# Attention results kept with 128 following positions in the partitions: fewer stores, longer loads, shorter shifted copies

## The chip, the cores and the metric

The kernel runs on one core of one Trainium2 chip. The metric is device time in microseconds (us) of one launch; the core's engines are TensorE (PE, its weight loads PEld), VectorE (DVE), ScalarE (ACT), GpSimd (POOL) and SyncE (SP), which here only issues DMAs.

## What is computed

Eight batches of eight heads, 576 positions, head dimension 64. Heads 0 to 3 attend to the last 32 positions, heads 4 to 7 to every fourth of the last 128. The results, 4608 tokens of 512 numbers, go through a mixture of eight experts in which each expert takes at most 576 tokens, assigned in the order of the sorted logits.

```python
scores = scale * np.matmul(q, k.transpose(0, 1, 3, 2))
rel = pos[:, None] - pos[None, :]
mask_plain = (rel >= 0) & (rel < 32)
mask_dil = (rel >= 0) & (rel < 128) & (rel % 4 == 0)
attn = softmax(np.where(mask, scores, -1e9))          # plain for h < 4, dilated for h >= 4
x = np.matmul(attn, v).transpose(0, 2, 1, 3).reshape(4608, 512)
logits = x @ w_gate                                    # greedy assignment, 576 tokens an expert
out[mask] = np.maximum(x[mask] @ w1[e], 0.0) @ w2[e]
```

## The kernel before

The launch has two parts. `attention` works through 32 units (class `Unit`): a batch has two kinds (0 plain, 1 dilated, whose sequence is stored as four runs of 144 positions, so that its window is also 32 following places), a kind two units of two heads. The sequence is cut into NB = 9 chunks of 64 positions. Per unit, `scan` (L447, L451) finds maxima on TensorE, VectorE reduces them (L398), `scores` (L458, L463) forms the scores, ScalarE takes the exponent (L417) into E, `values` (L470) multiplies by v, and `weigh` (L476 to L478) divides on VectorE into the tile xs. Head a of the unit lies in partitions 64a to 64a+63 of xs, with the nine chunks side by side. `banks` then transposes xs on TensorE (L519), copies the transposed results into xt (L264 on ScalarE, L524 for the very last) and feeds the gate's logits (L544; L608 and L610 in `tokens` for the last batch) and the first counts of the routing (`R.choose`: L840 to L850; coarse counts L726, L731).

`load` and `load_values` bring q, k and v in on SP's queue, with two sets of tiles taken in turn by the batches. v goes into partitions 64 to 127; `shift_v` (L274, L276) copies it to partitions 0 to 63 as two shifted copies, on GpSimd after the first batch, so that one matmul sees a chunk and the 32 places ahead of it.

`stores` (L491) writes xs to the scratch tensor xd in device memory: 2 DMAs a batch for kind 0, 20 for kind 1, since the dilated runs end inside chunks and each head half needs its own DMA. All of these are issued by SP, in program order, among the loads. SP's DMAs use eight landing semaphores in turn, and a DMA that reuses one waits until the eighth DMA before it has landed (`DMAHW0` to `DMAHW7` among the program's waits).

The order of the instructions on each engine is made at build time: `Schedule.run` simulates the engines with the costs that stand in the code (in ns) and due times (`P_U` a unit, and constants such as `B_V`, `B_K`), and writes each engine's program in the order that comes out. The three PSUM accumulators px are a `Pool` of three, shared by `values`, the transposes and the logits.

`moe` follows. It begins with `search_alone` (L804 and on), a chain between VectorE and TensorE that needs all counts; its tiles take memory of the attention's, so its first instruction also waits for all stores. The experts' matmuls (L1266, L1308) fill the rest.

Of the kernel before, what the change touches and what calls it, by code (L numbers as in the profile page):

```python
# [8 lines left out]
F32 = mybir.dt.float32  # L9
# [32 lines left out]
NS, B_E, DIRECT = (2, 2), 3000, 7  # L42
# [195 lines left out]
def attention(tc, ctx, C, load_const, T, xd, Lt, R):  # L238
# [11 lines left out]
    KT = [[pk.tile([128, 2, 32 + S], F32, name=f"k{x}{s}") for s in range(2)] for x in range(2)]  # L250
# [6 lines left out]
    XS = [ring(pk, [128, NB, 2, D], F32, f"xs{x}", NS[x]) for x in range(2)]  # L257
# [53 lines left out]
    def borders(kind, s, eng):  # L311
# [3 lines left out]
        def fn():  # L315
            e.memset(KT[kind][s][:, :, :32], 0.0)
            e.memset(VT[kind][s][:32, 0].rearrange("p h d -> p (h d)"), 0.0)
# [7 lines left out]
    def load(b, kind, part=None):  # L325
# [10 lines left out]
        lk = sp(1, lambda: nc.sync.dma_start(KT[kind][s][:, ix, 32:], k[b][:, ix]), load.old, nb, b)  # L336
# [15 lines left out]
    def load_values(b, kind):  # L352
# [3 lines left out]
        for part in range(2):  # L356
            eng = "POOL" if b else ("DVE", "ACT")[part]
            f = {"ACT": act, "DVE": nc.vector.tensor_copy, "POOL": nc.gpsimd.tensor_copy}[eng]
            ready["V", kind, b].append(op(eng, {"ACT": 2300, "DVE": 1700, "POOL": 2450}[eng],
                                          lambda part=part, f=f: shift_v(b, kind, part, f), [ld, ready["b", kind, s]],  # L360
                                          -4 * b * P_U))
# [3 lines left out]
    class Unit:  # L365


        def __init__(self, u):
# [10 lines left out]
            self.K = KT[kind][s][:, ui]  # L379
# [7 lines left out]
        def build(self):  # L387
# [39 lines left out]
            for g in range(2):  # L427
                c0, c1 = self.gr[g]
                px = Buf(PV)
                d = self.op("PE", 135 * (c1 - c0), lambda c0=c0, c1=c1, px=px: self.values(c0, c1, px.tile),  # L430
# [3 lines left out]
                x = self.op("DVE", 780, lambda c0=c0, c1=c1, px=px: self.weigh(c0, c1, px.tile, rec, xs),  # L434
# [31 lines left out]
        def values(self, c0, c1, px):  # L466
            px = px[:, :5 * (D + 1)].rearrange("p (c x) -> p c x", c=5)
            for c in range(c0, c1):
                for a in range(2):
                    nc.tensor.matmul(px[64 * a:64 * a + 64, c - c0], self.E[:, c, 64 * a:64 * a + 64],  # L470
                                     self.V[:, c, self.ui + 2 * a], start=True, stop=True)

        def weigh(self, c0, c1, px, rec, xs):
            m = c1 - c0
            px = px[:, :5 * (D + 1)].rearrange("p (c x) -> p c x", c=5)
            nc.vector.tensor_scalar(rec[:, c0:c1], px[:, :m, D], 1e-9, None, op0=OP.add)  # L476
            nc.vector.reciprocal(rec[:, c0:c1], rec[:, c0:c1])
            nc.vector.tensor_tensor(xs[:, c0:c1, self.ui], px[:, :m, :D], rec[:, c0:c1, None].to_broadcast([128, m, D]),  # L478
                                    op=OP.mult)
# [960 lines left out]
```

## Time and profile before

| | us |
|---|---|
| median of 3 runs (lowest, highest) | 720.73 (717.96, 721.19) |
| the profiled execution, its time | 728.06 |
| its span in the trace | 726.3 |
| attention until the last result is weighed | 0 to 217.3 |
| from there to the search's first instruction | 217.3 to 231.1 |
| search, first lists and gathers | 231.1 to 257.2 |
| experts | 257.2 to 726.3 |

Over the span TensorE is busy 90%, VectorE 66%, ScalarE 40%, GpSimd 27%. The granted clock of TensorE is given as a share of full speed; in the trace it is either full (2.4 GHz) or half (1.2 GHz), so a mean between says how long it was half. Idle time of an engine stands in brackets with what ended it.

### The profile page before, as it was taken

To read this page: it belongs to the slowest core of one execution; us is meant where nothing else is said; L and a number is where in the kernel's file an instruction comes from. 1 tells how busy PE (TensorE), PEld (TensorE's weight loads), DVE (VectorE), ACT (ScalarE), POOL (GpSimd) and SP (SyncE) were. 2 spreads that over 40 slices of the span, in tenths; PEclk is the share of its full clock that TensorE was granted. 3 is DMA by queue.
4 is the path that set the end of the run, shared out by engine and by line. 5 is a ranking of instruction groups with operands and counts; after the bars stand their busy time and mean duration, and the time that the engine had idled before them with its cause. 6 is when DMAs were issued, how large, how long until landed. Compare 5 with 4: busy or idle time off the path is not lost.

```text
span 726.3 us, 18691 instructions
## 1 busy us (share of the span) xinstructions
PE 651.2 (90%) x7447; PEld 558.5 (77%) x7449; DVE 477.3 (66%) x1551; ACT 288.9 (40%) x610; POOL 193.9 (27%) x231
## 2 busy tenths in 40 slices
PE   6879888787893389999999999999999999999995
PEld 4767776666772359879979988988988988988984
DVE  5566566657743878978959978978977973833300
ACT  4545443342340147457523524523533534434210
POOL 5362533432400033364320311221121041121011
PEclk7899999998796599999999999999999999999998
DMA  9995585784532168489712711622441374123001
GB/s 236 272 232 163 156 220 159 179 197 111 131 80 54 45 196 174 111 260 225 232 54 68 246 51 52 197 102 66 151 147 52 131 254 152 60 75 100 1 23 43
DMA packets 67095, 99.07 MB, mean 136 GB/s; under 512 B 8000, under 2 KB 36416, under 8 KB 67008
## 3 DMA queue, kind: packets, MB, share of 16 engines
q1 hardware_dynamic: 57664, 72.71, 35.7%
q0 software_dynamic: 9344, 25.17, 13.0%
q8 instruction: 58, 0.95, 0.6%
q14 instruction: 29, 0.24, 0.1%
HBM read 72.69 MB, written 18.87 MB: 126 GB/s over the span
## 4 chain that ended last, share of the span: by engine, by line
PE 62%; DVE 15%; issue 14%; DMA 4%; SPq 2%; POOL 2%; ACT 1%; POOLq 0%; DVEq 0%
PE ph L1266 18%; PE py L1308 17%; PE pS L463 5%; PE px L470 4%; DMA k<-in_kp 4%; PE px L519 2%; PE px L544 2%; PE ptx L1229 2%; PE pz L739 2%; PE pS L458 2%; PE pm L451 1%; SPq L491 1%; PE py L1311 1%; PE py L1313 1%; DVE hb L1286 1%
## 5 line engine op out<-in xcount | busy, mean ns | idle before, releaser
L1308 PE MATMUL py<-w2h,hb 128*128 128x512 f32 x512 | 171.1, 399 | 0.0
L1266 PE MATMUL ph<-xh,w1h 128*128 128x256 f32 (+1 forms) x512 | 138.0, 300 | 0.0
L1266 PE MATMUL ph<-xl,w1h 128*128 128x256 f32 (+1 forms) x512 | 136.7, 298 | 0.0
L1266 PE MATMUL ph<-xh,w1l 128*128 128x256 f32 (+1 forms) x512 | 135.9, 296 | 0.0
L1308 PEld LDWEIGHTS py<-w2h,hb 128*128 128x128 f32 x512 | 96.1, 188 | 19.2
L1308 PE MATMUL py<-w2l,hb 128*128 128x512 f32 x256 | 99.9, 390 | 0.0
L1098 ACT ACTIVATE hb<-ph 128x256 fp32r<-128x256 f32 (+2 forms) x192 | 59.6, 345 | 89.3 <-PE ph L1266 87.0
L1334 POOL DMA_INDIRECT out<-y,idx x40 | 39.9, 997 | 197.1 <-ACT y L1098 138.3
L1266 PEld LDWEIGHTS ph<-xh,w1h 128*128 128x128 f32 x512 | 91.8, 190 | 0.5
L1266 PEld LDWEIGHTS ph<-xh,w1l 128*128 128x128 f32 x512 | 91.7, 190 | 0.1
L1266 PEld LDWEIGHTS ph<-xl,w1h 128*128 128x128 f32 x512 | 91.4, 190 | 0.1
L417 ACT ACTIVATE E<-pS 128x384 f32<-128x384 f32 x96 | 46.5, 490 | 89.4 <-PE pS L463 79.3
L1286 DVE SCALAR_TENSOR_TENSOR hb<-ph,hb 128x320 fp32r<-128x320 f32 (+1 forms) x128 | 57.1, 453 | 28.1 <-ACT hb L1098 25.0
L1098 ACT ACTIVATE y<-py 128x512 f32<-128x512 f32 (+1 forms) x40 | 23.8, 596 | 102.1 <-PE py L1308 90.3
L463 PE MATMUL pS<-q,k 128*64 128x64 f32 x1152 | 58.6, 244 | 3.1 <-issue 3.1
L1215 POOL DMA_INDIRECT xg<-xd,idx x40 | 41.6, 1040 | 51.9 <-PE ph L1266 31.4
L1308 PEld LDWEIGHTS py<-w2l,hb 128*128 128x128 f32 x256 | 48.2, 188 | 8.4
L1098 ACT ACTIVATE w1h<-raw 128x512 fp32r<-128x512 f32 x64 | 40.0, 629 | 34.7 <-DVE oa L1031 28.8
L470 PE MATMUL px<-v,E 128*64 128x65 f32 x1152 | 49.2, 240 | 4.0 <-issue 4.0
L463 PEld LDWEIGHTS pS<-q,k 128*64 128x64 f32 x1152 | 49.5, 154 | 3.5 <-issue 3.5
L470 PEld LDWEIGHTS px<-v,E 128*64 128x64 f32 x1152 | 43.6, 153 | 10.2 <-issue 8.7
L274 POOL COPY v<-v 32x2080 f32<-32x2080 f32 x14 | 26.9, 1920 | 82.5 <-DMA v<-in_vp 56.7
(190 smaller groups left out, 1103.0 us busy)
## 6 DMA issues: line engine op xcount, KB each, us to landing
raw<-in_moe_w SPq DMA_DIRECT2D x128, 256.0 KB, 4.4
v<-in_vp SPq DMA_DIRECT2D x8, 585.0 KB, 10.3
v<-in_vd SPq DMA_DIRECT2D x8, 585.0 KB, 12.3
xd<-xs SPq DMA_DIRECT2D x16, 288.0 KB, 6.5
w2l<-raw POOLq DMA_DIRECT2D x16, 256.0 KB
qs<-in_qp SPq DMA_DIRECT2D x7, 576.0 KB, 10.0
k<-in_kp SPq DMA_DIRECT2D x7, 576.0 KB, 17.8
qs<-in_qd SPq DMA_DIRECT2D x7, 576.0 KB
```

Source lines behind the costliest of these rows:

```text
L274: f(t[:32, 1:], t[96:, :NB - 1])
L417: e = self.op("ACT", 490, lambda j=j, pS=pS: nc.scalar.activation(self.E[:, 3 * j:3 * j + 3].rearrange("p c x -> p (c x)"), pS.tile[:, :38 ...
L458: nc.tensor.matmul(pS[64 * h:64 * h + 64, k, :, h], self.ls[:64 + NB, 3 * j + k], self.r[:64 + NB, 64 * h:64 * h + 64], start=(k == 0), st ...
L463: nc.tensor.matmul(pS[64 * h:64 * h + 64, k, :, h], self.K[:, 32 * g:32 * g + 64], self.Q[:, g], start=False, stop=True, skip_group_check= ...
L470: nc.tensor.matmul(px[64 * a:64 * a + 64, c - c0], self.E[:, c, 64 * a:64 * a + 64], self.V[:, c, self.ui + 2 * a], start=True, stop=True)
L519: nc.tensor.transpose(t[:, c], xs[:, 3 * i + c].rearrange("p a d -> p (a d)"), C["identf"])
L1098: act = lambda o, i, f=AF.Copy: nc.scalar.activation(o, i, f)
L1215: nc.gpsimd.indirect_dma_start(out=xg[:n], out_offset=None, in_=xd, in_offset=bass.IndirectOffsetOnAxis(ap=box[0][:n, m:m + 1], axis=0))
L1266: nc.tensor.matmul(o, a[:, d * 128:d * 128 + 128], b[:, d, c0:c1], start=((d, i) == pairs[0]), stop=((d, i) == pairs[-1]))
L1286: hl = op("DVE", 335 if j == 0 else 400, lambda: nc.vector.scalar_tensor_tensor(hb[:, CAP + c0:CAP + c1], o, 0.0, hb[:, c0:c1], op0=OP.max ...
L1308: nc.tensor.matmul(py, x, w, start=(f + i == 0), stop=(f == NF - 1 and i == 2))
L1334: s = nc.gpsimd.indirect_dma_start(out=out, out_offset=bass.IndirectOffsetOnAxis(ap=box[0][:n, m:m + 1], axis=0), in_=y[:n], in_offset=None)
```

## The change

A unit now takes two heads that stand next to each other (2ui and 2ui+1), and xs has 128 following positions in the partitions, five columns of four heads each: two chunks make a column, the fifth holds one chunk. `values` makes four matmuls a column, two for its two chunks and two for the heads, also in the fifth, where the second half repeats chunk 8 and is not used; that is 20 a unit, where 18 stood. A store row has four heads (1024 bytes, where 512 stood), and a batch has 2 stores for kind 0 and 8 for kind 1. The transposes run in each unit, five of 128 x 128 (the fifth 64 x 128) in two PSUM tiles, where nine per kind stood in three. k lies as one run of 1152 a partition, v is read as one run of 9360 bytes a partition, and `shift_v` copies three chunks at a time.

```diff
-NS, B_E, DIRECT = (2, 2), 3000, 7
+NS, B_E, DIRECT, V_ST = (2, 2), 3000, 7, 3
...
-    KT = [[pk.tile([128, 2, 32 + S], F32, name=f"k{x}{s}") for s in range(2)] for x in range(2)]
+    KT = [[pk.tile([128, 32 + 2 * S], F32, name=f"k{x}{s}") for s in range(2)] for x in range(2)]
...
-    XS = [ring(pk, [128, NB, 2, D], F32, f"xs{x}", NS[x]) for x in range(2)]
+    XS = [ring(pk, [128, 5, 4, D], F32, f"xs{x}", NS[x]) for x in range(2)]
...
     def load_v(b, kind):
-        src = T["in_vp" if kind == 0 else "in_vd"]
-        nc.sync.dma_start(VT[kind][b % 2][64:].rearrange("p c h d -> p c (h d)"),
-                          src[b].rearrange("(c i) x -> i c x", i=64))
-
-    def shift_v(b, kind, part, f):
+        nc.sync.dma_start(VT[kind][b % 2][64:].rearrange("p c h d -> p (c h d)"), T["in_vp" if kind == 0 else "in_vd"][b])
+
+    def shift_v(b, kind, part, f, c0, c1):
         t = VT[kind][b % 2].rearrange("p c h d -> p c (h d)")
         if part == 0:
-            f(t[:32, 1:], t[96:, :NB - 1])
+            c1 = min(c1, NB - 1)
+            f(t[:32, c0 + 1:c1 + 1], t[96:, c0:c1])
         else:
-            f(t[32:64], t[64:96])
+            f(t[32:64, c0:c1], t[64:96, c0:c1])
...
-        lk = sp(1, lambda: nc.sync.dma_start(KT[kind][s][:, ix, 32:], k[b][:, ix]), load.old, nb, b)
+        kx = slice(32, 32 + 2 * S) if part is None else slice(32 + S * part, 32 + S * part + S)
+        lk = sp(1, lambda: nc.sync.dma_start(KT[kind][s][:, kx], k[b][:, ix].rearrange("p u n -> p (u n)")), load.old, nb, b)
...
-            self.gr = ((0, 5), (5, 9))
+            self.gr, self.gv = ((0, 5), (5, 9)), ((0, 3), (3, 5))
...
-                    usex.append(op("SP", 475 if kind == 0 else 100, f, Unit.xsd, -u * P_U - 5000, dma=rows * 512 / D_R))
-            banks(self, xs, list(Unit.xsd), usex)
+                    usex.append(op("SP", 475, f, Unit.xsd, -u * P_U - 5000, dma=rows * 512 / D_R))
+            banks(self, xs, Unit.xsd[-2:], usex)
...
         def values(self, c0, c1, px):
-            px = px[:, :5 * (D + 1)].rearrange("p (c x) -> p c x", c=5)
+            px = px[:, :6 * (D + 1)].rearrange("p (c a x) -> p c a x", c=3, a=2)
             for c in range(c0, c1):
                 for a in range(2):
-                    nc.tensor.matmul(px[64 * a:64 * a + 64, c - c0], self.E[:, c, 64 * a:64 * a + 64],
-                                     self.V[:, c, self.ui + 2 * a], start=True, stop=True)
+                    for h in range(2):
+                        k = min(2 * c + h, NB - 1)
+                        nc.tensor.matmul(px[64 * h:64 * h + 64, c - c0, a], self.E[:, k, 64 * a:64 * a + 64],
+                                         self.V[:, k, 2 * self.ui + a], start=True, stop=True)
...
-        runs = [(0, NB, 0, 64, 0, 0)] if kind == 0 else [
-            (0, 2, 0, 64, 0, 0), (2, 1, 0, 16, 0, 128), (2, 1, 16, 64, 1, 0), (3, 1, 0, 64, 1, 48), (4, 1, 0, 32, 1, 112),
-            (4, 1, 32, 64, 2, 0), (5, 1, 0, 64, 2, 32), (6, 1, 0, 48, 2, 96), (6, 1, 48, 64, 3, 0), (7, 2, 0, 64, 3, 16)]
-        for c, n, i0, i1, r, t in runs:
-            for a in range(2):
...
+        if kind == 0:
+            put(0, 4, 0, 128, 0, 128)
+            put(4, 1, 0, 64, 512, 1)
+            return out
+        for c in range(5):
+            n = 128 if c < 4 else 64
+            cut = 16 * c
+            for i0, i1 in ((0, cut), (cut, n)) if c < 4 else ((0, n),):
+                if i1 > i0:
+                    r, t = divmod(128 * c + i0, SR)
+                    put(c, 1, i0, i1, DIL * t + r, 1)
...
-        for i in range(3 if ui else 0):
+        for i, (c0, c1) in enumerate(((0, 2), (2, 5))):
...
-            t = un.op("PE", 420, turn, done, late, pt)
+            t = un.op("PE", 95 + n * 109 // 128, turn, done[:i + 1], late, pt)
```

Here `put(c, n, i0, i1, first, step)` stores partitions i0 to i1 of n columns from c on, with rows of four heads. `weigh` is written for the new shape with the same three instructions per group, and in `tokens` the logits of head pair g wait for xt[2g] and xt[2g+1] alone. The layout of q, k and v on the host is changed to match, and v's becomes contiguous by partition.

Three places show how the programs' orders differ. The first is SP's queue in the middle of the attention: the loads and kind-1 stores of one batch up to the k load of a later one (xs_125 is the results tile of odd batches, k_95 the keys' tile of even ones). Before:

```order
L336 DMA k_98<-in_kd 128x2x576
L268 DMA v_106<-in_vd 64x9x260
L491 DMA xd<-xs_125 64x2x128 x4
L491 DMA xd<-xs_125 64x128 x4
L491 DMA xd<-xs_125 48x128 x4
L491 DMA xd<-xs_125 32x128 x4
L491 DMA xd<-xs_125 16x128 x4
L335 DMA qs_110<-in_qd 128x1152
L336 DMA k_95<-in_kp 128x2x576
```

And with the change:

```order
L336 DMA k_98<-in_kd 128x1152
L267 DMA v_106<-in_vd 64x2340
L492 DMA xd<-xs_125 128x256
L492 DMA xd<-xs_125 112x256
L492 DMA xd<-xs_125 96x256
L492 DMA xd<-xs_125 80x256
L492 DMA xd<-xs_125 64x256
L334 DMA qs_110<-in_qd 128x1152
L492 DMA xd<-xs_125 48x256
L492 DMA xd<-xs_125 32x256
L492 DMA xd<-xs_125 16x256
L336 DMA k_95<-in_kp 128x1152
```

The k load still stands behind the stores of that batch, but behind 8 where 20 stood.

The second place is SP's queue at the end of the attention, the last batch's results up to the first read of the router's choice (eidx). Before:

```order
L491 DMA xd<-xs_123 64x9x128 x2
L491 DMA xd<-xs_125 64x2x128 x2
L491 DMA xd<-xs_125 16x128 x2
L491 DMA xd<-xs_125 48x128 x2
L491 DMA xd<-xs_125 64x128 x2
L491 DMA xd<-xs_125 32x128 x4
L491 DMA xd<-xs_125 64x128 x2
L491 DMA xd<-xs_125 48x128 x2
L491 DMA xd<-xs_125 16x128 x2
L491 DMA xd<-xs_125 64x2x128 x2
L1344 TENSOR_LOAD eidx
```

And with the change, with the semaphores that each row waits for (DVE for a weighed group, DMAHW for a landing):

```order
L492 DMA xd<-xs_123 128x4x256 [waits DMAHW2_49,DVE_49]
L492 DMA xd<-xs_123 64x256 [waits DMAHW3_49]
L492 DMA xd<-xs_125 128x256 [waits DMAHW4_49,DVE_49]
L492 DMA xd<-xs_125 16x256 [waits DMAHW5_49]
L492 DMA xd<-xs_125 112x256 [waits DMAHW6_49]
L492 DMA xd<-xs_125 32x256 [waits DMAHW7_49]
L492 DMA xd<-xs_125 96x256 [waits DMAHW0_49]
L492 DMA xd<-xs_125 48x256 [waits DMAHW1_49,DVE_49]
L492 DMA xd<-xs_125 80x256 [waits DMAHW2_49]
L492 DMA xd<-xs_125 64x256 [waits DMAHW3_49]
```

Five of the last eight stores now wait for the last unit's first weighed group only, and three for its second.

The third place is GpSimd's program, the shifted copies of one v load (v_103) and the q copies beside them. Before:

```order
L347 COPY q_99<-qs_107 64x18x32 x3
L274 COPY v_103<-v_103 32x2080
L276 COPY v_103<-v_103 32x2340
```

And with the change:

```order
L347 COPY q_99<-qs_107 64x18x32 x3
L273 COPY v_103<-v_103 32x780 x2
L273 COPY v_103<-v_103 32x520
L275 COPY v_103<-v_103 32x780 x3
```

The copies keep their place behind the q copies; two instructions have become six.

## Rows read from the trace of the kernel before

**Rows 1.** Four stages: us, engines' busy us (x), PEclk, DMA share, GB/s.

```profile
0.00:217.30 217.30, 179.09 (x3986) 145.13 (x3987) 132.26 (x414) 89.07 (x170) 80.93 (x77) 0.88 0.71 178
217.30:231.10 13.80, 3.97 (x39) 2.52 (x39) 2.93 (x14) 1.07 (x3) 0.00 (x0) 0.71 0.33 77
```

**Rows 2.** SP's issues, 128 to 182 us: start, us, line, what.

```profile
129.64 19.09 SPq L491 DMA_DIRECT2D xd<-xs  x20
148.84 0.35 SPq L335 DMA_DIRECT2D qs<-in_qd  x1
149.29 0.60 SPq L336 DMA_DIRECT2D k<-in_kp  x1
...
175.00 0.60 SPq L336 DMA_DIRECT2D k<-in_kp  x1
```

**Rows 3.** The stores' line as a whole: issue ns min/median/max.

```profile
L491 SPq DMA_DIRECT2D xd<-xs x176: 302/452/4312, 33.5 to 228.5; - x176
```

**Rows 4.** Timeline of TensorE with its idle time before, two places.

```profile
157.29 0.35 PE L451 MATMUL pm<-k,q 128*64 128x64 bf16 x10 [2.68 <-DMA k<-in_kp]
...
179.24 0.48 PE L451 MATMUL pm<-k,q 128*64 128x64 bf16 x10 [2.97 <-DMA k<-in_kp]
```

**Rows 5.** The two stretches around them, columns as in 1.

```profile
155.00:165.00 10.00, 7.71 (x168) 6.99 (x169) 6.43 (x23) 4.20 (x9) 4.11 (x2) 0.83 1.08 238
175.00:185.00 10.00, 7.03 (x142) 4.88 (x142) 5.35 (x17) 0.51 (x2) 0.74 (x1) 0.81 0.88 247
```

**Rows 6.** Chain of waits at the attention's end: start, us, what.

```profile
216.89 0.44 DVE xs L478
217.33 0.60 SPq L491
...
228.46 2.11 DMA xd<-xs
```

**Rows 7.** Timeline at the same place, idle time and releaser in brackets.

```profile
220.64 0.36 DVE L618 COPY L<-px 128x192 f32<-128x192 f32 x1 [1.67 <-PE px L610]
...
223.33 1.00 PE L731 MATMUL pz<-oh,pre 128*128 128x8 bf16 x10 [1.72 <-DVE pre L726]
231.12 0.17 DVE L804 TENSOR_SCALAR_CACHE_REDUCE junkc<-pz 128x8 f32<-128x8 f32 x1 [7.06 <-DMA xd<-xs]
```

**Rows 8.** Chain of waits, two TensorE pieces at full clock.

```profile
204.51 1.20 PE px L470 x36
...
207.76 1.13 PE px L519 x9
```

**Rows 9.** Groups by shape, attention: busy us, mean ns, idle before.

```profile
L276 POOL COPY v<-v 32x2340 f32<-32x2340 f32 x14 | 29.9, 2138 | 0.7
...
L264 ACT ACTIVATE xt<-px 128x384 f32<-128x384 f32 x46 | 21.7, 490 | 26.3 <-PE px L519 18.5 <-DVE mx L398 3.1 <-DVE rec L476 2.8
...
L478 DVE TENSOR_TENSOR xs<-px,rec 128x320 f32<-128x320 f32 x32 | 15.7, 492 | 1.6
...
L347 POOL COPY q<-qs 64x576 f32<-64x576 f32 x21 | 14.1, 670 | 30.3 <-DMA qs<-in_qp 29.4
```

**Rows 10.** Timeline of VectorE and GpSimd in one routing step.

```profile
112.63 0.17 DVE L842 TENSOR_SCALAR key<-M 128x4 int32<-128x4 int32 x1
112.66 1.92 POOL L274 COPY v<-v 32x2080 f32<-32x2080 f32 x1 [4.62 <-DMA v<-in_vd]
112.83 1.76 DVE L843 TENSOR_TENSOR key<-M,key 128x4 int32<-128x4 int32 x1
...
114.62 2.13 POOL L276 COPY v<-v 32x2340 f32<-32x2340 f32 x1
114.63 2.15 DVE L845 CAST V<-key 128x4 f32<-128x4 uint16 x1
```

**Rows 11.** DMA view, 66.5 to 67.5 us (k's rows), 68.5 to 70.0 (v's).

```profile
DMA packets 165, 0.38 MB, mean 380 GB/s; under 512 B 0, under 2 KB 0, under 8 KB 165
...
DMA packets 289, 0.30 MB, mean 200 GB/s; under 512 B 0, under 2 KB 289, under 8 KB 289
```

More of the change, by code (lines that the diff above doesn't have):

```diff
@@ L315, in fn @@
         def fn():
-            e.memset(KT[kind][s][:, :, :32], 0.0)
+            e.memset(KT[kind][s][:, :32], 0.0)
             e.memset(VT[kind][s][:32, 0].rearrange("p h d -> p (h d)"), 0.0)
@@ L358, in load_values @@
             f = {"ACT": act, "DVE": nc.vector.tensor_copy, "POOL": nc.gpsimd.tensor_copy}[eng]
-            ready["V", kind, b].append(op(eng, {"ACT": 2300, "DVE": 1700, "POOL": 2450}[eng],
-                                          lambda part=part, f=f: shift_v(b, kind, part, f), [ld, ready["b", kind, s]],
-                                          -4 * b * P_U))
+            step = V_ST if b else NB
+            for c in range(0, NB, step):
+                ready["V", kind, b].append(op(eng, {"ACT": 255, "DVE": 190, "POOL": 275}[eng] * step,
+                                              lambda part=part, f=f, c=c: shift_v(b, kind, part, f, c, c + step),
+                                              [ld, ready["b", kind, s]], -4 * b * P_U))
     load.q = None
@@ L486, in stores, with put @@
-        for c, n, i0, i1, r, t in runs:
-            for a in range(2):
-                x = xd[b * S:(b + 1) * S, 256 * kind + 128 * a:256 * kind + 128 * a + 128]
-                if kind:
-                    x = x.rearrange("(t r) x -> r t x", r=DIL)[r, t:t + n * (i1 - i0)]
-                out.append((lambda x=x, c=c, n=n, i0=i0, i1=i1, a=a: nc.sync.dma_start(
-                    x.rearrange("(c i) x -> i c x", c=n),
-                    xs[64 * a + i0:64 * a + i1, c:c + n].rearrange("p c a d -> p c (a d)")), n * (i1 - i0)))
+        def put(c, n, i0, i1, first, step):
+            row = (DIL if kind else 1) * DM
+            o = xd.offset + (b * S + first) * DM + 256 * kind
+            out.append((lambda: nc.sync.dma_start(
+                bass.AP(tensor=xd.tensor, offset=o, ap=[[row, i1 - i0], [step * DM, n], [1, 256]]),
+                xs[i0:i1, c:c + n].rearrange("p c h d -> p c (h d)")), 2 * n * (i1 - i0)))
@@ L512, in banks, with turn, keep @@
         xt, oldt, uset = xt_[b, kind]
[L513 removed]
+        for i, (c0, c1) in enumerate(((0, 2), (2, 5))):
             pt = Buf(PV)
[L516 to L525 removed]
+            n = min(128 * c1, S) - 128 * c0
+            def turn(c0=c0, c1=c1, pt=pt):
+                for c in range(c0, c1):
+                    m = 128 if c < 4 else 64
+                    nc.tensor.transpose(pt.tile[:, 128 * (c - c0):128 * (c - c0) + m],
+                                        xs[:m, c, 2 * ui:2 * ui + 2].rearrange("p a d -> p (a d)"), C["identf"][:m, :m])
+            end = b == B - 1 and (kind, ui, i) == (1, 1, 1)
+            def keep(c0=c0, n=n, pt=pt, act=nc.vector.tensor_copy if end else act):
+                act(xt[:, ui, 128 * c0:128 * c0 + n], pt.tile[:, :n])
             late = B_K if b < B - 1 else B_E
[L528 removed]
+            t = un.op("PE", 95 + n * 109 // 128, turn, done[:i + 1], late, pt)
             usex.append(t)
[L530 removed]
+            k = un.op("DVE" if end else "ACT", 100 + n, keep, [t, *oldt], late)
             pt.users.append(k)
@@ L610, in logits @@
             nc.tensor.matmul(pt.tile[:32, 128:128 + t0], wgp[:, g], text(b, g, 0, t0), start=False, stop=(g == 3), skip_group_check=True)
-        t = un.op("PE", 330, lambda: logits(0), [*xt_[b][:3], ready["w"]], late, pt)
-        t = un.op("PE", 330, lambda: logits(1), [t], late)
-        t = un.op("PE", 330, lambda: logits(2), [t, *xt_[b]], late)
-        t = un.op("PE", 330, lambda: logits(3), [t], late)
+        t = ready["w"]
+        for g in range(4):
+            t = un.op("PE", 330, lambda g=g: logits(g), [t, *xt_[b][2 * g:2 * g + 2]], late, *([pt] if g == 0 else []))
         for kk in range(2):
```

32 lines of the change are left out of this document (12 added, 20 removed).

## The prediction, made before the result was known

> **What bounds the kernel now.** I first cut the span into stages [rows 1]. Through the attention, 217.3 us, TensorE is busy 179.1 us (82%) at a mean clock of 0.88, so it is the engine that sets the pace, with 38.2 us in which it does nothing. In the 13.8 us behind it TensorE works 4.0 us and the DMA engines are busy a third: there something else is waited for. What comes later (search, experts) is not touched by the change.
>
> Then I looked at SP, since the change takes work from its queue. The block of 20 stores of a kind-1 result holds SP from 129.64 to 148.73 us, and a k load is issued right behind it, at 149.29 [rows 2]. An issue of a store takes 0.45 us in the median [rows 3], so twenty need 9.0 of the 19.1 us; the rest is waiting for landings, eight DMAs back. The reader is to see that the k load isn't late because the DMA engines are full, but because it stands behind stores. Its price is on TensorE's timeline: 2.68 and 2.97 us idle until k has landed, for the loads issued at 149.29 and 175.00 [rows 4]. Around these two gaps the clock's mean is 0.83 and 0.81 over ten us [rows 5], so the clock was at its lower level for some 3.4 and 3.8 us, in which matmuls take twice as long: another 1.7 and 1.9 us lost.
>
> The last look is at the end of the attention. The chain of waits goes from the last weighing, which ends at T = 216.89 + 0.44 = 217.33, through the stores' issues to the landing of the last one at 228.46 + 2.11 = 230.57 [rows 6]. VectorE's first instruction of the search follows at 231.12, having waited 7.06 us for that store, while the other path, logits and coarse counts, is done at 223.33 + 1.00 = 224.33 [rows 7].
>
> **The change, part by part.** The sum is made in the time of the profiled execution: span 726.3, its own time 728.06, so 1.8 us lie outside. The median of the runs is 7.3 us below that; I carry the difference over to it unchanged.
>
> 1. The end. Eight stores follow where twenty stood, and only three of them wait for the last weighed group. If all eight are issued behind T at the dearest price of the chain's rows, 0.60, the last lands at 217.33 + 4.8 + 2.11 = 224.2; if three at 0.45 stand behind T, at 220.8. The other path then decides, 224.33 or a little earlier: behind T there are three transposes, not six (0.126 each [rows 8]), and logits of one head pair, not two. I take 223.5, and the search starts as long behind it as now: 230.57 - 223.5 = 7 us saved. Bounds: 6.2 (that path not shortened) and 8.
>
> 2. The k loads. Twelve stores fewer, at 0.45 each, are 5.4 us by which the load is issued earlier, before any landing wait is counted; it has to be 2.7 to 3.0 earlier. So both gaps should close: 5.65 us. Of the 3.6 us of slow clock I count two thirds, since other short gaps stand near. That is 8 us; bounds 0 (another late input stands right behind) and 9.3. Other loads also stand in SP's queue, and idle time of TensorE that these two gaps don't explain is 32 us; I give it 2 us, bounds 0 and 15.
>
> 3. TensorE's own work. Twenty matmuls a unit for 18 are 64 more, at 1.20/36 = 0.033 us [rows 8]: +2.1. Ten transposes per kind and batch for nine, with the same number of columns in all: 16 more, between nothing and 0.126 each; I take +0.5. Together +2.6, bounds 1.3 (half in idle time) and 4.1.
>
> 4. VectorE and ScalarE. The larger group's product has 384 columns where 320 took 0.492 us [rows 9]; in proportion 0.59, or +0.1 a unit, 3.1 in all, on an engine that is busy 132 of 217 us. ScalarE copies the same number of transposed columns in four pieces per kind and batch for three; a whole piece takes 0.49, so 16 more are at most 7.8 us on an engine busy 89. Waiting for matmuls covers both: nothing; without this cover of VectorE's, +3.1.
>
> 5. The shifted copies. GpSimd takes 2.138 us for 2340 columns and 0.670 for 576 [rows 9], so 0.83 ns a column and 0.19 us fixed. A piece of 780 is then 0.84, one of 520 is 0.62, and the six of a load 4.8 us where two take 4.1: +0.76 for each of 14 loads, 10.6 us of an engine with over 130 us idle. But these copies also stop VectorE. In a routing step an instruction of four columns takes 0.17 us (L842), while L843 and L845 beside the copies take 1.76 and 2.15, and each ends where a copy ends [rows 10]; 3.6 us are lost there. If each waits for a piece instead, the loss is 1.7, so 1.9 are saved; if the instructions behind them each meet the next piece, it can become all six pieces, 4.8, or 1.2 more than now. The row is one step of some, and I take -0.5 in all, bounds -6 and +4 (three such steps, and a little). The Trainium skill ("SBUF — State Buffer", section "Who interferes with whom") says that VectorE and GpSimd share a port pair as an exclusive lock: the one that comes second is blocked for the whole of the other's instruction. The trace agrees: 112.66 + 1.92 is 114.58, and L843 ends at 114.59. By the rule alone, a wait per instruction, the step gives -1.9; by the longer list of instructions behind it, up to +1.2, which is why I don't count it as a gain.
>
> 6. The long v loads. While only k's long rows move the DMA engines do 380 GB/s, while only v's rows of 1040 bytes move 200 GB/s [rows 11]. At these rates a v load of 599 KB takes 3.0 us, at k's rate it would take 1.6. No gap of TensorE that I read ends with v, so I count nothing; 1.4 us a load would matter only for the third rival below. The Trainium skill (same page, section "Door 1: The DMA port swizzle") has a rule that speaks against this part: partitions 64 to 127 reach 8 of the 16 ports, whatever the length of a row. The trace's half rate agrees, though there rows are short too. By it v stays near 200 GB/s, and I hold that rival's chance lower for it.
>
> Sum: -7 - 8 - 2 + 2.6 - 0.5 = -14.9 us, so 711 for the span and 720.73 - 14.9 = 706 for the median.
>
> **The rivals.**
> A, my forecast, 55%: 699 to 713.
> B, 20%: only the end is gained. k comes earlier, but q's copies, VectorE or the PSUM accumulators are what TensorE then waits for in the same place; the order of every engine is new, so there is room for that. -7 + 2.6 - 0.5 = -4.9, 716 (714 to 718). For it: k's waits are only 5.65 us of 38. Against: k is what ended both gaps [rows 4].
> C, 14%: SP was behind with everything, and with 16 issues a batch for 28 half of the 38.2 idle us goes: -19 - 7 + 2.6 = -23, 697 (690 to 701). Against: much of that idle time isn't SP's in any row I read, and v's rate.
> D, 7%, the slower one: six pieces instead of two, and v landing earlier, while the routing step runs. Each load whose whole 4.8 us falls into VectorE's chain costs that much; one such step stands in my rows. From three more of them (14.4 us) the gain of 14.9 is gone; with six more it is +14, 735. Against: a piece is short, and GpSimd pauses between loads.
> E, 4%: the new stores are not cheaper to issue because each covers up to 128 partitions and 512 rows; at twice 0.45 a store the end gains some 4 us and k 1.5, and 718 results. Against: the q load with 128 rows is issued in 0.35 us, the k load with two runs in each of 128 partitions in 0.60 [rows 2].
>
> **How the numbers follow.** The point is A's. Below 695 lies a third of C, 5%; above 717 lie D, most of E and a little of B, some 12%: so 695 to 717. A measurement of this kernel tells 0.5%, 3.6 us, from no change. Faster than 717.1 are A, C, most of B (17 of 20) and 1 of E: 87%. Within 3.6 us: 3 of B, 2 of E and 2 of D, 7%. Slower: 6%.
>
> **What would show it.** Right: the search's first instruction waits for counts or a store at about T + 6.5 us, not T + 13.8; SP's kind-1 block of 8 stores takes 8 to 12 us; no idle time on TensorE ends with k after the first batch; six copies a load on GpSimd of 0.84 and 0.62 us; VectorE's L843 and L845 (12 or 13 lines further down) below 1 us each. Wrong: T itself is not before 212 us although k is on time (B); a routing step longer than 5 us on VectorE (D); store issues near 1 us (E).

## The result, and the profile after

The changed kernel takes 714.69 us in the median of 20 runs (lowest 707.75), the kernel before 725.2 in 20 runs beside it. The ratio is 0.9866 [0.9834, 0.9898], a gain of 1.0 to 1.7%. Ratios here and below leave out executions more than 1.5% slower than the fastest of the same kernel beside them, which is why 0.9866 is not 714.69 / 725.2, why one execution of the changed kernel (811.67 us) doesn't count, and why the last row of the table below has no T. The forecast was 706 us with a range of 695 to 717, made from a median of 720.73, that is a ratio of 0.980 (0.964 to 0.995). The measured ratio, 0.9866, lies inside this range, on its slower side. The profiled execution has a span of 713.5 us where before had 726.3: 12.8 us less, where my sum said 14.9.

The same two stages as in [rows 1], with T the end of the last weighing (columns: us, busy us of PE, PEld, DVE, ACT, POOL with instruction counts, granted clock, DMA share, GB/s):

```profile
0.00:211.20 211.20, 185.47 (x4143) 146.46 (x4144) 127.12 (x414) 91.90 (x186) 88.43 (x133) 0.94 0.68 185
211.20:217.80 6.60, 3.12 (x28) 1.75 (x26) 2.89 (x14) 0.56 (x2) 0.00 (x0) 0.80 0.32 92
```

The attention is 6.1 us shorter and the stage behind it 7.2 us; from the search on nothing changed (726.3 - 231.1 = 495.2 us before, 713.5 - 217.8 = 495.7 now). The reader is to see two things in the first row. TensorE is idle for 25.7 us of the attention where it was idle for 38.2. And yet it is busy for 6.4 us more than before, although its clock was slow for less of the time (0.94 for 0.88). Forecast was an idle time 7.7 us shorter, and a busy time about the same (2.4 less for the clock, 2.6 more for the work).

The end, on the timeline (start, us, engine, line; the idle time before an instruction and what ended it in brackets), beside [rows 6, 7]:

```profile
210.36 5.31 SPq L492 DMA_DIRECT2D xd<-xs  x8
...
210.82 0.42 DVE L483 TENSOR_TENSOR xs<-px,rec 128x256 f32<-128x256 f32 x1
...
216.16 1.00 PE L744 MATMUL pz<-oh,pre 128*128 128x8 bf16 x10 [1.72 <-DVE pre L739]
217.80 0.17 DVE L817 TENSOR_SCALAR_CACHE_REDUCE junkc<-pz 128x8 f32<-128x8 f32 x1 [0.91 <-DMA xd<-xs]
```

T is 210.82 + 0.42 = 211.24 and the search starts 6.56 us later, where it started 13.8 us later. The counts end at 216.16 + 1.00 = 217.16, and the chain of waits has the last store from 213.56 to 217.26, so both paths now end together. Two more executions of the changed kernel (below) have the counts last.

SP's queue in the middle of the attention, beside [rows 2]:

```profile
136.74 6.82 SPq L492 DMA_DIRECT2D xd<-xs  x8
143.89 0.39 SPq L336 DMA_DIRECT2D k<-in_kp  x1
...
161.11 17.66 SPq L492 DMA_DIRECT2D xd<-xs  x10
```

A block of eight stores takes 6.8 us where twenty took 19.1, and the k load behind it is issued at once. The 17.66 us of the last row are SP waiting for results that aren't there yet: the queue has run ahead of the attention. What TensorE waits for from 28 to 205 us (engine, line, releaser: us in total, times, longest), first two lines of before, then the longest of the changed kernel:

```profile
PE pm L451 <- DMA k<-in_kp: 6.1, 3, 3.0
PE px L519 <- DVE xs L478: 5.1, 3, 3.3
```

```profile
PE px L474 <- issue: 7.7, 5, 3.0
PE pS L460 <- ACT E L419: 2.5, 1, 2.5
PE pm L449 <- DVE R L407: 2.0, 2, 1.1
PE pm L405 <- DVE mx L400: 1.7, 2, 1.2
```

No wait for k is left in that stretch, where [rows 4] had two of nearly 3 us. The transposes' wait for the weighing (L519 before) is gone too.

The shifted copies are as forecast. GpSimd's groups by shape, then VectorE and GpSimd on the timeline of one routing step, beside [rows 9, 10]:

```profile
L275 POOL COPY v<-v 32x780 f32<-32x780 f32 x42 | 33.7, 836 | 0.7
L273 POOL COPY v<-v 32x780 f32<-32x780 f32 x28 | 22.7, 833 | 28.9 <-DMA v<-in_vd 15.4 <-DMA v<-in_vp 13.1
...
L273 POOL COPY v<-v 32x520 f32<-32x520 f32 x14 | 8.6, 614 | 0.0
```

```profile
155.98 0.23 DVE L855 TENSOR_SCALAR key<-M 128x4 int32<-128x4 int32 x1
156.22 2.42 POOL L275 COPY v<-v 32x780 f32<-32x780 f32 x3
156.24 0.82 DVE L856 TENSOR_TENSOR key<-M,key 128x4 int32<-128x4 int32 x1
157.10 0.76 DVE L858 CAST V<-key 128x4 f32<-128x4 uint16 x1
```

L856 and L858, the lines that took 1.76 and 2.15 us, now wait for one piece each.

### The profile page after: what moved, and what is told of

Same layout as the page of the kernel before. It is cut to its first block, busy times and chain, and to the rows that moved or that the text cites. A ratio compares the mean times of both kernels' runs of the same rounds, so it can differ in the third digit from the quotient of the medians.

```text
span 713.5 us, 19000 instructions
## 1 busy us (share of the span) xinstructions
PE 658.5 (92%) x7591; PEld 559.3 (78%) x7593; DVE 471.0 (66%) x1551; ACT 290.9 (41%) x626; POOL 204.0 (29%) x287
## 4 chain that ended last, share of the span: by engine, by line
PE 57%; DVE 14%; issue 13%; DMA 10%; POOL 2%; ACT 1%; SPq 1%; POOLq 0%; DVEq 0%
PE py L1321 16%; PE ph L1279 16%; PE px L474 5%; PE pS L465 3%; PE px L533 3%; DMA qs<-in_qp 2%; DMA raw<-in_moe_w 2%; DMA qs<-in_qd 2%; PE ptx L1242 2%; PE px L558 2%; PE pz L752 2%; DVE hb L1299 1%; PE py L1324 1%; PE py L1326 1%; DMA k<-in_kd 1%
## 5 line engine op out<-in xcount | busy, mean ns | idle before, releaser
L1347 POOL DMA_INDIRECT out<-y,idx x40 | 42.5, 1063 | 195.9 <-ACT y L1111 137.3
L474 PE MATMUL px<-v,E 128*64 128x65 f32 x1280 | 51.9, 234 | 7.8 <-issue 7.7
L465 PE MATMUL pS<-q,k 128*64 128x64 f32 x1152 | 56.5, 239 | 0.9 <-issue 0.9
L474 PEld LDWEIGHTS px<-v,E 128*64 128x64 f32 x1280 | 46.1, 147 | 13.6 <-issue 11.5
L1228 POOL DMA_INDIRECT xg<-xd,idx x40 | 41.6, 1040 | 52.7 <-PE ph L1279 25.7
L465 PEld LDWEIGHTS pS<-q,k 128*64 128x64 f32 x1152 | 47.5, 149 | 1.1 <-issue 1.0
L1112 DVE TENSOR_TENSOR w2l<-raw,w2h 128x512 fp32r<-128x512 f32 x48 | 32.0, 685 | 22.7 <-ACT w2h L1111 22.3
```

The costliest lines, as they stand in the source:

```text
L465: nc.tensor.matmul(pS[64 * h:64 * h + 64, k, :, h], self.K[:, 32 * g:32 * g + 64], self.Q[:, g], start=False, stop=True, skip_group_check= ...
L474: nc.tensor.matmul(px[64 * h:64 * h + 64, c - c0, a], self.E[:, k, 64 * a:64 * a + 64], self.V[:, k, 2 * self.ui + a], start=True, stop=True)
L1112: sub = lambda e, o, a, b: e.tensor_tensor(o, a, b, op=OP.subtract)
L1228: nc.gpsimd.indirect_dma_start(out=xg[:n], out_offset=None, in_=xd, in_offset=bass.IndirectOffsetOnAxis(ap=box[0][:n, m:m + 1], axis=0))
L1347: s = nc.gpsimd.indirect_dma_start(out=out, out_offset=bass.IndirectOffsetOnAxis(ap=box[0][:n, m:m + 1], axis=0), in_=y[:n], in_offset=None)
```

## The experiments

Ratios are to the kernel before, run beside each. T and the search's start are from each one's trace (us).

| kernel | median | ratio [95%] | T | search |
|---|---|---|---|---|
| changed (the result) | 714.69 | 0.9866 [0.9834, 0.9898] | 211.24 | 217.80 |
| changed again, first | 712.6 | 0.979 [0.9737, 0.9843] | 209.17 | 215.50 |
| twenty stores | 726.01 | 0.9977 [0.9935, 1.0019] | 215.93 | 227.72 |
| twenty at the end | 716.49 | 0.9849 [0.9791, 0.9907] | 208.22 | 219.99 |
| whole copies | 716.19 | 0.9828 [0.9763, 0.9892] | 208.39 | 214.44 |
| short v rows | 716.18 | 0.9876 [0.9824, 0.9929] | 209.27 | 215.58 |
| no repeat | 713.98 | 0.9814 [0.9762, 0.9867] | 208.33 | 214.48 |
| stores on two queues | 715.04 | 0.9855 [0.9808, 0.9902] | 207.82 | 214.00 |
| before, two queues | 727.52 | 1.0001 [0.9964, 1.0038] | 216.18 | 229.09 |
| changed again, second | 716.74 | 0.9843 [0.9768, 0.9918] | 210.59 | 216.71 |
| full transposes | 713.36 | 0.9812 [0.9744, 0.988] | 206.22 | 212.37 |
| halves apart | 727.17 | 1.0026 [0.9961, 1.0091] | 221.93 | 227.98 |
| before, short copies | 730.46 | 0.9993 [0.9936, 1.005] | - | - |

My theory was that the twenty stores in SP's queue cost the time, at the end and ahead of the k loads, and that the rest of the change is worth little. The rivals: the long v rows or the short copies carry part of it, or TensorE's own work, made cheaper or dearer, decides. All variants keep the order of the instructions of the kernel that they are made from, but for the edit. They were run in three groups. The changed kernel stands again in the first group (with twenty stores, twenty at the end and whole copies) and in the last (with full transposes, halves apart and before with short copies). Short v rows, no repeat and the two runs on two queues have none beside them, and are compared with all of its executions.

**Changed again** (no edit), twice, to see how far executions of one program differ.

> The changed kernel itself, as a control for the runs beside it: 0.987 of before within the interval of the first measurement (0.983 to 0.990), the last result weighed at about 211 us, the search begun 6.6 us behind that.

> The changed kernel once more, as the measure for the others of this call: ratio 0.977 to 0.990, T between 208 and 211.5 us by all theories.

T was 209.17 and 210.59, and 211.24 above. Two variants below, twenty at the end and stores on two queues, change nothing before the last batch's stores, and have 208.22 and 207.82: so one and the same attention spans 207.82 to 211.24, and a T inside these 3.4 us tells nothing. The three ratios reach from 0.979, below what was expected for it, to 0.9866, and the forecast 0.980 lies at the favourable end of them.

**Twenty stores.** The changed kernel, with each kind-1 result stored in 20 DMAs of rows of 512 bytes.

```diff
-            out.append((lambda: nc.sync.dma_start(
-                bass.AP(tensor=xd.tensor, offset=o, ap=[[row, i1 - i0], [step * DM, n], [1, 256]]),
-                xs[i0:i1, c:c + n].rearrange("p c h d -> p c (h d)")), 2 * n * (i1 - i0)))
...
+                for p0, p1 in ((i0, i0 + 64), (i0 + 64, i1)) if i1 - i0 > 100 else ((i0, i1),):
+                    for a in range(2):
+                        nc.sync.dma_start(
+                            bass.AP(tensor=xd.tensor, offset=o + (p0 - i0) * row + 128 * a, ap=[[row, p1 - p0], [1, 128]]),
+                            xs[p0:p1, c, 2 * a:2 * a + 2].rearrange("p h d -> p (h d)"))
```

> Every kind-1 result of the changed kernel is stored with 20 DMAs of 512-byte rows again, issued at the same places of the same program order; all else is as changed. Theory 1 (the stores in SP's queue hold both gains): the end gets back 12 issues of 0.45 to 0.6 us, 5.4 to 7 us, and the k loads are again issued 5 us or more later, so TensorE waits for k once or twice for 2 to 4 us; 10 us (7 to 14) more than the changed kernel, a ratio to before of 0.997 to 1.007. Theory 2 (the gain within the attention comes from the short copies, the long loads or the new order): the end alone is given back, 6 us more, ratio 0.994 to 0.997, the last result weighed at 211 us still.

The gain is gone. On the timeline SP's block is long again, the k load stands behind it, and TensorE waits for k:

```profile
147.81 17.57 SPq L501 DMA_DIRECT2D xd<-xs  x20
165.48 0.37 SPq L336 DMA_DIRECT2D k<-in_kp  x1
```

```profile
172.27 0.35 PE L453 MATMUL pm<-k,q 128*64 128x64 bf16 x10 [3.58 <-DMA k<-in_kp]
```

The stretch up to T, for the idle time of TensorE (columns as above):

```profile
0.00:215.90 215.90, 184.69 (x4144) 144.96 (x4144) 126.22 (x414) 91.93 (x186) 88.82 (x133) 0.97 0.67 181
```

Against the changed kernel run beside it, T is 6.8 us later (4.7 to 8.1 against the five T's above) and the way from T to the search 5.5 us longer (11.79 for 6.33), which is the difference between the two spans (723.0 - 711.0 = 12.0) within 0.3 us. So the stores are the cause, in both places. The edit also halves their rows; at the end it is their number that counts, since the chain there is one issue after the other (next run), and in the middle number and row length are not told apart.

**Twenty at the end.** The same edit in the last batch alone (`b == B - 1`).

> Only the last batch's kind-1 result is stored with 20 DMAs of 512-byte rows, the earlier seven with 8. Both theories: the stores behind the last weighing end 5.4 to 7 us later, so the search begins 12 to 13.5 us behind the last weighing in place of 6.6; 6 us more than the changed kernel, ratio to before 0.994 to 0.997. A rival of this: if the end is held by the counts and not by the stores, nothing changes, ratio 0.987.

T stays with the changed kernel's and the search starts 11.77 us behind it, 5.4 more than with eight. The whole time shows less of it than expected: 0.9849 where 0.994 to 0.997 was, with an interval that overlaps the changed kernel's 0.979. The chain of waits (start, us, what) is SP's issues again, then the last landing:

```profile
217.35 0.47 SPq L501
217.87 1.97 DMA xd<-xs
219.99 0.19 DVE junkc L828 x2
```

This tells the two places apart: of the 12.0 us, 5.4 belong to the end and the rest, within the spread of T, to the stores of the batches before.

**Whole copies** and **before, short copies.** The shifted copies in one piece in the changed kernel, and in pieces of three chunks in the kernel before.

```diff
# changed kernel, whole copies
-                                              lambda part=part, f=f, c=c: shift_v(b, kind, part, f, c, c + step),
+                                              lambda part=part, f=f, c=c: c == 0 and shift_v(b, kind, part, f, 0, NB),
# kernel before, short copies
+        step = 3 if b else NB
+        for c in range(0, NB, step):
+            if part == 0:
+                d = min(c + step, NB - 1)
+                f(t[:32, c + 1:d + 1], t[96:, c:d])
+            else:
+                f(t[32:64, c:c + step], t[64:96, c:c + step])
```

> The shifted copies of v are made whole again, two of about 2 us in place of six of 0.6 to 0.85, at the places of the same program order; all else is as changed. Theory 1 (stores in SP's queue): VectorE's routing instructions that meet a copy wait up to 2.1 us again, some of it in the chain, 0 to 4 us more than the changed kernel, ratio 0.987 to 0.992. Theory 2a (the short copies hold the attention's gain): 6 us more, ratio 0.995. If short copies only add waits for VectorE: 1 to 3 us less, ratio 0.983 to 0.986.

> The kernel before with one part of the change alone: the values' shifted copies on GpSimd in pieces of three chunks. If the pieces are worth next to nothing for the time (my term 5), VectorE's longest blocked instructions fall from about 2 us to below 1, T stays within 215.5 to 218 us, and the ratio is 0.995 to 1.003. If part of the changed kernel's gain came from them, the ratio is below 0.995. If VectorE meets one piece after the other (rival D), T is 219 us or more and the ratio above 1.003.

With whole copies VectorE's routing instructions are blocked again:

```profile
150.93 2.12 DVE L856 TENSOR_TENSOR key<-M,key 128x4 int32<-128x4 int32 x1
```

But neither tells from its neighbour: 0.9828 beside 0.979 with overlapping intervals, T 208.39 within the spread; and 0.9993 for the pieces alone. So what VectorE loses to the copies costs no time that these runs can show.

**Short v rows.** The changed kernel with v read in rows of 1040 bytes, as before.

```diff
-        nc.sync.dma_start(VT[kind][b % 2][64:].rearrange("p c h d -> p (c h d)"), T["in_vp" if kind == 0 else "in_vd"][b])
+        nc.sync.dma_start(VT[kind][b % 2][64:].rearrange("p c h d -> p c (h d)"),
+                          T["in_vp" if kind == 0 else "in_vd"][b].rearrange("(c i) x -> i c x", i=64))
```

> The changed kernel with v loaded in rows of 1040 bytes as before; order and queues as changed. If the long v loads are worth nothing (my term 6: partitions 64 to 127 stay near 200 GB/s whatever the row), T stays within 208 to 212 us and the ratio to the kernel before within 0.977 to 0.988, as the changed kernel has it. If the long rows carry a part of the gain of T (the rival), each of the loads lands later, T is 3 us or more later than 211.2, and the ratio is 0.988 to 0.995.

T is 209.27, as with long rows, and the ratio's interval overlaps those of the changed kernel. The long rows buy no time here, and they are not seen to move faster either. [rows 11] had 200 GB/s for v's short rows and 380 for k's. In the DMA view, with hardly anything but v under way, the changed kernel's long rows show 192 GB/s from 162 to 164 us and 253 in the second of these two us, and the short rows of this run 250 from 163.5 to 165 us:

```profile
DMA packets 41, 0.38 MB, mean 192 GB/s; under 512 B 0, under 2 KB 0, under 8 KB 0
...
DMA packets 27, 0.25 MB, mean 253 GB/s; under 512 B 0, under 2 KB 0, under 8 KB 0
```

```profile
DMA packets 364, 0.38 MB, mean 250 GB/s; under 512 B 3, under 2 KB 364, under 8 KB 364
```

**No repeat.** The changed kernel without the multiplication that repeats chunk 8: 18 matmuls a unit for 20. (The unused half is filled once ahead of the attention; that part of the edit isn't shown.)

```diff
-                        k = min(2 * c + h, NB - 1)
+                        k = 2 * c + h
+                        if k == NB:
+                            continue
```

> The changed kernel without the second multiplication of chunk 8 (18 matmuls of values a unit for 20), whose place in the accumulator is filled once with ones; the values that are stored don't change, as that half is never stored. If TensorE's own work sets the pace (term 3 at its full size), 64 matmuls of 0.033 us are 2.1 us, T is near 208 and the ratio 0.003 lower than the changed kernel's (0.976 to 0.984). If the work is hidden in idle time of TensorE (lower bound of term 3), T moves by less than 1 us and the ratio is as changed.

T is 208.33, which decides nothing: it is near the 208 that term 3 at its full size gives, and within the spread of T as well. What decides is on TensorE's timeline, which has two rows for each of these matmuls (1152 rows of L470 before, for 32 units of 18). The second group of a unit, with 16 rows in the changed kernel, and here with 12:

```profile
204.95 0.69 PE L474 MATMUL px<-v,E 128*64 128x65 f32 x16
```

```profile
206.70 0.68 PE L476 MATMUL px<-v,E 128*64 128x65 f32 x12
```

A quarter of the matmuls fewer, and 0.01 us less: in this group the repeat costs next to nothing, and my price of 0.033 us was wrong for it.

**Halves apart.** The same 20 matmuls, all into partitions 0 to 63 first, then all into 64 to 127.

```diff
-            for c in range(c0, c1):
-                for a in range(2):
-                    for h in range(2):
+            for h in range(2):
+                for c in range(c0, c1):
+                    for a in range(2):
```

> The changed kernel with the loops of the value matmuls turned: all that write partitions 0 to 63 of a group first, then all that write 64 to 127, instead of the two halves by turns; the same matmuls, the same number. If two neighbouring matmuls into different halves run side by side, so that a pair costs what one would (then the repeated chunk costs nothing beside its partner and the price in term 3 was that of a pair), 20 matmuls a unit need 20 places of 0.13 us instead of 10: up to 1.3 us in each of 32 units, T 25 to 42 us later, ratio 1.01 to 1.04. If every matmul costs its own time wherever it writes (term 3 as I worked it out), T and the ratio stay as changed.

T is 221.93, 11.6 us later than the mean of the three executions of the changed kernel (210.3), and the gain on the kernel before is gone. The first group of a unit in the changed kernel (its second, of 0.69 us, stands above), then both groups here:

```profile
203.96 0.92 PE L474 MATMUL px<-v,E 128*64 128x65 f32 x24
```

```profile
213.05 1.44 PE L474 MATMUL px<-v,E 128*64 128x65 f32 x24
...
214.56 0.97 PE L474 MATMUL px<-v,E 128*64 128x65 f32 x16
```

So neighbours that write different halves do run side by side, and only their order was changed. The size was well below my 25 to 42: these two groups grow by 0.52 + 0.28 = 0.80 us, not 1.3, and over the attention it is less. In the stretch up to T (columns as above; the changed kernel run beside it, then this one) TensorE is busy 17.0 us longer, and its idle time, 20.2 us for 26.0, takes a part of that:

```profile
0.00:210.60 210.60, 184.63 (x4143) 145.35 (x4144) 128.51 (x414) 92.34 (x186) 90.32 (x133) 0.96 0.66 186
```

```profile
0.00:221.90 221.90, 201.67 (x4143) 163.95 (x4144) 128.16 (x414) 91.75 (x186) 88.75 (x133) 0.98 0.64 177
```

**Full transposes.** The fifth transpose of a unit over 128 partitions; the lower half, the repeated chunk, is not copied on.

```diff
-                    m = 128 if c < 4 else 64
+                    m = 128
```

> The changed kernel with the transpose of the last chunk taken over all 128 partitions; its lower half holds the repeated chunk 8 and the copy behind it leaves it out, so the results are the same, and no instruction is added or taken away. In the changed kernel two transposes of 128 partitions and one of 64 take 0.57 us from the first start to the next matmul, where before nine of 128 took 1.14. If the one of 64 partitions costs 0.15 to 0.19 more than one of 128 would, and TensorE sets the pace (term 3, which I then made too small), 32 units save 4.8 to 6 us of T and the ratio is 0.006 to 0.008 below the changed kernel's of this call. If that time is hidden in TensorE's idle time (term 3 as I sized it), T and the ratio stay as changed within 0.002.

T is 206.22, the earliest of all, 4.1 us before the changed kernel's mean but only 1.6 before the earliest T of the same attention (207.82). TensorE's own time tells more: busy 176.30 us up to T, for 184.63 in the changed kernel run beside it, at the same clock of 0.96. On the timeline a group of two full transposes and the 64-partition one, and the next matmul behind it, in the changed kernel, then here; and five together (the changed kernel's three are from its second repetition, where the same instruction follows):

```profile
200.26 0.64 PE L533 MATMUL px<-const,xs 128*128 128x128 f32 x3
200.83 0.44 PE L579 MATMUL px<-const,L 128*128 128x128 f32 x2
```

```profile
207.07 0.86 PE L533 MATMUL px<-const,xs 128*128 128x128 f32 x5
207.86 0.28 PE L460 MATMUL pS<-R,const 73*64 73x64 bf16 x6
```

```profile
196.23 0.55 PE L533 MATMUL px<-const,xs 128*128 128x128 f32 x3
196.61 0.38 PE L579 MATMUL px<-const,L 128*128 128x128 f32 x2
...
202.15 0.77 PE L533 MATMUL px<-const,xs 128*128 128x128 f32 x5
202.84 0.28 PE L460 MATMUL pS<-R,const 73*64 73x64 bf16 x6
```

```profile
0.00:206.20 206.20, 176.30 (x4143) 140.74 (x4144) 127.93 (x414) 90.97 (x186) 88.83 (x133) 0.96 0.68 190
```

From start to next start three take 0.38 us for 0.57, five 0.69 for 0.79: with the last transpose over twice as many rows a group is 0.10 to 0.19 us cheaper. In 32 units that is 3.2 to 6.1 us, and the 4.1 us by which T is earlier agree with it, though T's spread is nearly as large. The whole time doesn't settle it: 0.9812 beside 0.9843 for the changed kernel, with overlapping intervals.

**Stores on two queues**, in the changed kernel (every second store of the last kind-1 result) and in the kernel before (ten of its twenty), from ScalarE's queue.

```diff
# changed kernel
+            q = nc.scalar if kind and b == B - 1 and len(out) % 2 else nc.sync
-            out.append((lambda: nc.sync.dma_start(
+            out.append((lambda: q.dma_start(
# kernel before
+                q = nc.scalar if kind and b == B - 1 and a else nc.sync
```

> The changed kernel with every second store of the last kind-1 result issued from ScalarE's queue. If the stores' issue on SP is still what ends last behind T, the last store lands 1.5 to 2 us sooner and the search starts at T + 5 to 5.5 instead of T + 6.3 to 6.6, when the path of logits and counts takes over: ratio 0.001 to 0.002 below the changed kernel's. If that other path is already as late as the stores, the search starts at T + 6.1 or later and nothing moves. If ScalarE's issues delay its copies of the transposed results, which stand in the same queue, the search starts at T + 7 or later.

> The kernel before, with ten of the twenty stores of the last kind-1 result issued from ScalarE's queue; nothing else is changed. If the 13.8 us behind T come from the number of issues in one queue (my term 1), the search starts at T + 7 to 9.5, where the path of logits and counts decides, and the ratio is 0.991 to 0.994 with T unchanged near 217. If they come from the stores' landing (DMA engines, or the memory that they write), halving the issues per queue leaves T + 12 or more and the ratio at 0.998 to 1.002.

In the changed kernel the search starts 6.18 us behind T, as before the edit, and its first instruction waits for the counts, as it does in both repetitions without the edit:

```profile
214.00 0.17 DVE L818 TENSOR_SCALAR_CACHE_REDUCE junkc<-pz 128x8 f32<-128x8 f32 x1 [0.53 <-PE pz L745]
```

So the stores have nothing more to give at that place. In the kernel before the edit gained nothing, T + 12.9, against my theory's T + 7 to 9.5, but it isn't the test that I meant it to be. The queues wait for each other: SP's waits and ScalarE's (line, releaser: us in total, times, longest) show a store of SP's held for 5.0 us by a landing, and ScalarE's copy of the last logits 4.3 us behind the stores in its queue. The last landing ends the chain:

```profile
SPq L492 <- DMA xd<-xs: 6.7, 4, 5.0
```

```profile
ACT Lt L264 <- DMA xd<-xs: 4.3, 1, 4.3
```

```profile
226.43 2.11 DMA xd<-xs
```

That is T + 12.4, where before had T + 13.2.

Whether twenty stores on two truly separate queues would do is left open; that twelve fewer do is shown by the two runs with twenty stores.

## Why the prediction came out as it did

The mechanism was right where the gain comes from, the stores in SP's queue, and the gain somewhat smaller than forecast. That the sum came so near is in part luck, since two of its errors offset each other (points 2 to 4). Point by point:

1. **The end**, forecast -7: measured 13.8 - 6.56 = -7.2. The size is right, the steps less so. Three stores wait for the last weighing, but the issues of five start behind T. The last of them takes 2.1 us, where I took 0.60 for the dearest (the chain of before also has one of 1.39), and lands at T + 6.0; the counts end at T + 5.9, near the T + 6.2 of the sum. So the other path took over only narrowly. The number of stores alone gives 5.4 of the 7.2 (twenty at the end). With twenty stores the search starts 2.0 us sooner behind T than in the kernel before; no run tells why.
2. **The k loads**, forecast -8, and -2 for other loads. The direction is shown by the run with twenty stores, and the size was too large: the stores ahead of the loads are worth 6.8 us of T, not 10. TensorE's idle time in the attention did fall by 38.2 - 25.7 = 12.5 us, not 7.7, but the stores explain less than half of it: with the same order and twenty stores it is 215.9 - 184.7 = 31.2 us, so some 7 us of the relief don't come from them. One part has a name: before, the transposes waited 5.1 us for the weighing, and with the change, where each unit has its own, no such wait is listed for them; with twenty stores it is 0.2 us. That is read from the waits; no run changes it alone. SP's block of eight took 6.8 us, a little less than the 8 to 12 that were to show the forecast right.
3. **TensorE's own work**, forecast +2.6 (1.3 to 4.1): this is the step that failed, "64 more, at 1.20/36 = 0.033 us" and "between nothing and 0.126 each". First, the 36 rows are 18 matmuls, so the price of one alone would have been 0.067, and +4.3 for 64. Second, it isn't a price for one: neighbours in different halves share their time, so before a unit had nine pairs and now has ten, and the repeated chunk is free. The chain of waits has these pieces now, beside [rows 8] and two pieces of before (first) that stand at the same places:

```profile
211.87 0.62 PE px L470 x16
...
215.03 0.61 PE px L470 x20
```

```profile
205.02 0.62 PE px L474 x16
...
207.14 0.79 PE px L533 x5
...
208.52 0.73 PE px L474 x24
```

   The values take 0.73 + 0.62 = 1.35 us a unit for 0.61 + 0.62 = 1.23, which is +3.8 in 32 units. Third, the transposes are not priced by columns: twice 0.79 stands where nine took 1.13, +0.45 a kind and batch, +7.2 in sixteen; 3.2 to 6.1 us of TensorE's time came back when the fifth transpose was made a full one. Together about +11, where I had +2.6. Of the first point the Trainium skill has the rule ("TensorEngine Tiling (Array Packing)", section "Tiling Modes"): an array of 128 x 64 is two tiles that load weights and multiply independently; the runs agree, 0.92 us for 12 matmuls by turns and 1.44 with the halves apart. The same section says that a change of the tiling mode drains TensorE; the 0.10 to 0.19 us that a group loses by its 64-partition transpose agree with that. By these two rules the repeat would have been free and the fifth transpose dear.
4. **T** came out 6.1 us earlier (8.2 and 6.7 in the two other executions), where the sum for it, with the copies, said 7.9. That is near, but because two errors offset each other: 12.5 us of idle time less instead of 7.7, and 6.4 us of busy time more instead of none. If the work grew by 11, the rest, 4.6 us, is the clock (0.94 for 0.88, where I had counted 2.4). This last split is worked out, not tested; the kernel before on two queues, whose attention is the same but for its last stores, was busy 176.2 us up to T at a clock of 0.93, and beside it the changed kernel's 183.6 and 185.5 at 0.94 make the work +7 to +9. The two errors also hang together: TensorE's idle time is least where its work was made most (20.2 us, halves apart) and 29.9 with full transposes, so some of the idle time that is gone was filled with the added work.
5. **VectorE and ScalarE**, forecast nothing: right. Nor did the weighing's larger product matter (0.56 us, forecast 0.59).
6. **The copies**, forecast -0.5: pieces of 0.84 and 0.61 us as worked out, each wait one piece long, no effect on the time in either direction.
7. **The long v loads**, forecast nothing: right. The Trainium skill's rule on partitions 64 to 127 ("SBUF — State Buffer", section "Door 1: The DMA port swizzle"), on which term 6 drew, agrees with the trace in kind: long or short, v's rows stay at 192 to 253 GB/s, far below k's 380.

Of the rivals, B (only the end) would be a ratio of 716/720.73 = 0.993, outside the interval, and its mark, T not before 212 us, did not come, by less than 1 us in the profiled execution; A's 699 to 713 are 0.970 to 0.989, which holds it. But B has a core of truth: the transposes and values took back about what k's gaps gave. C's relief of idle time is there in part (12.5 of its 19) but TensorE's own work took half of it back. D and E had no trace: no routing step longer than before, and a store's issue of 0.424 us in the median.

## What to carry to other kernels

Count DMAs in a queue before bytes: twelve stores fewer a batch gave 5.4 us at the end, where a chain waits for them, and 6.8, within 4.7 to 8.1, ahead of loads that stand behind them. When a change re-shapes small matmuls on a saturated engine, price them from start to next start in their new neighbourhood: whether two neighbours write different halves, and whether the tile's shape changes, moved more time here than the number of matmuls. And when the sum comes out right, look at each term's own row, since idle time off by 5 us and busy time off by 6 nearly cancelled here.

## What the runs showed of the hardware that was not expected

A transpose of 64 partitions among transposes of 128 made a group 0.10 to 0.19 us longer than a full one in its place. Twenty matmuls took 1.35 us a unit when neighbours wrote different halves of the partitions, and up to 0.80 us more in the other order. Stores in ScalarE's queue and in SP's waited for each other: halving a queue's share of twenty stores brought the last landing only from T + 13.2 to T + 12.4. And what is left of TensorE's waiting is mostly "issue": at one line 7.7, 3.7 and 11.4 us in the three executions of the changed kernel, 15.3 in the one with twenty stores; what holds the engine there was not tried.
